# Attention and a squared-ReLU feed-forward layer on one core: q loaded in 1 KB rows, and two more products done with seven half-size products for eight

## The chip, the cores and the metric

The kernel runs on one core of a Trainium2 chip. The metric is the time of one execution on the device in microseconds (us), as the median of several runs. A profile of one execution gives the rest: a core has TensorE (PE; its weight loads are listed as PEld), VectorE (DVE), ScalarE (ACT), GpSimd (POOL), SyncE (SP), which here only issues transfers, and sixteen DMA engines. PE writes to PSUM, which here is cut into two double banks, `strip0` and `strip1`, and four single banks, `ps0` to `ps3`.

## What is computed

The reference, cut to what matters (B = H = 8, S = 576, 16 beacon tokens, D = 64, 4608 tokens, d_model = 512, d_ff = 2048):

```python
k_all = np.concatenate([beacon_k, k], axis=2)          # 592 keys
v_all = np.concatenate([beacon_v, v], axis=2)
scores = scale * np.matmul(q, k_all.transpose(0, 1, 3, 2))
scores = np.where(causal, -1000000000.0, scores)       # beacons are always seen
a = softmax(scores)
x = np.matmul(a, v_all).transpose(0, 2, 1, 3).reshape(4608, 512)
h = np.maximum(x @ w_in, 0.0)
out = (h * h) @ w_out
```

## The kernel before

**Attention.** It goes batch by batch (eight batches), and within a batch by four pairs of heads. Scores are computed with keys on the partitions and queries along the columns (`score_mm`, line 676): the two heads of a pair lie on partitions 0 to 63 and 64 to 127, so a pair's two matmuls use the two halves of the array side by side. `SEGS` lists the causal pieces of a pair (key tile, first and last query), 1664 columns in all. They are put one after the other into strips of 512 columns (`add_stream`), ACT takes the exponential from PSUM into `pt` (line 786), DVE masks the diagonal tiles (line 808), PE multiplies by V with a column of ones (A.V, line 830), DVE divides (lines 848 and 850) and writes `xn`.

**Loads.** For batches 2 to 7 (`b >= NPE`) q, k and v are loaded from SP in tiles of 128 tokens by 8 heads (`add_load`, line 440), in rows of 64 floats, which are 256 bytes. There are six buffers `stg`. POOL casts them to bf16 (line 396), and DMA transposes, issued from SP (`add_trans`, line 472), bring 20 tiles of 128 x 128 of q and as many of k into `qT` and `kT`. Batches 0 and 1 load from POOL's queue or, for the very first tokens, from SP and ACT (`add_first_loads`, line 583), and are transposed by PE. `xn` becomes `xT` by PE for batches 0 to 2, and by DMA transposes from SP (line 882) for the others. `xT` is a ring of 1728 tokens.

**Feed-forward.** The 4608 tokens are nine chunks of 512. A chunk's first product is x by w_in (64 matmuls of 512 columns, line 1143; a chunk that crosses the ring's end has each matmul split in two), then ReLU (lines 1159 and 1161) and square (lines 1169 and 1171). Its second product is by w_out. There are two forms of each:

- Plain. The second product in this form is on line 1194, for chunks below `FAST` = 2.
- Seven for eight. The matrices are cut in quarters and seven products of half size take the place of eight, after sums of quarters made by DVE. For the second product (line 1257) this holds for chunks 2 to 8; the sums of the activations are on line 1228, the evacuations on lines 394 and 1281, the differences of weights on line 944. For the first product it holds for chunks from `BOTH` = 7 on, that is 7 and 8 (`add_first_both`, matmuls on line 1017). POOL copies the chunk out of `xT` (`pull`), DVE makes four sums of it (line 995) and once four of w_in (line 959). One chain of four products (`x`: 1, 6, 7, 4) runs in a strip, read out between the products by ACT or DVE (line 394), the others (`z`: 2; `y`: 5, 3) in a `ps` bank, read out by DVE additions (line 1065). ReLU and square follow on lines 1090 to 1098. These products use memory of the attention: the sums of w_in and the pulled chunk lie in `qk_area`, which holds q and k of the last batches, others in `pt` and `stg`.

**What sets the order.** Each step is an `Op` with a priority, dependencies, and the buffers it takes and gives back. `Order.run` plays a plan of the engines in which every op has a length, and puts the instructions of each engine down in the order that comes out; at run time each engine works its list in that order. Tables refine the plan: `NUDGE` shifts priorities by name, `HOME` fixes an engine. A chunk's ops are added after the batch that completes its tokens (`late`, at the end). The streams of scores are held back by how far the feed-forward work has come (`gate_at`), so that the two kinds of work are interleaved on PE: attention keeps ACT, DVE and the DMA engines busy while PE works on chunks.

Of the kernel before, what the change touches and what calls it, by code (L numbers as in the profile page):

```python
# [17 lines left out]
    "fldk0": 658.071, "fldk1": 538.534, "fcq3": -23.8, "bkl0": 22.188, "ek0.0.0": -25.42, "tp0.0.1k": -476.9,  # L18
    "eq0.0.3": -51.138, "tp0.1.0k": -975.238, "eq0.1.0": -201.003, "tp0.1.1k": 92.697, "ek0.1.1": -17.465,
    "tp0.1.2k": -1278.23, "ek0.1.3": -50.758, "eq0.1.3": 210.345, "qk2.1.0": -1322.85, "qk3.1.0": -1576.95,  # L20
    "qk3.1.2": 98696.4, "xte0.0.1": 72.837, "xte0.0.2": 202.007, "xtp0.1.1": 1543.7, "xtp0.1.3": 299.523,
    "tp1.0.0k": -36.734, "tp1.0.2q": 99521.3, "tp1.0.3k": 99518.5, "mask4.0.2": -52.183, "exp5.7.-1.1.0": -4.503,
    "exp5.7.0.0.0": 466.023, "qk6.10": 99505.4, "exp6.10.-1.0.0": 90.776, "exp6.10.-1.1.0": 79.415,
    "exp6.10.1.0.1": 147.224, "exp7.13.-1.1.0": -161.243, "xte1.0.2": 65.923, "s1.0.0.0": -97989.7,
    "relu0.0.0": 0.295, "s1.0.1.0": -98820.7, "relu0.0.1": 179.265, "sq0.0.1": 54.421, "s1.0.2.0": -300.425,
    "s1.0.3.0": -98822.7, "s1.0.2.1": -118.835, "s1.0.3.1": 8.01, "relu0.3.1": -97.929, "sq0.1.1": -91.845,
    "s1.0.8.1": -99593.7, "sq0.4.1": -12.447, "s1.0.11.0": -100291.234, "relu0.10.1": -97.474,
    "s1.0.11.1": -100375.057, "sq0.5.1": -107.919, "sq0.2.0": -108.607, "s1.0.4.1": 45.995, "s1.0.5.1": -257.73,
    "s1.0.6.0": -12.465, "s1.0.7.0": 328.542, "s1.0.6.1": 126.896, "relu0.6.1": 736.189, "s1.0.12.0": -261.69,
    "s1.0.12.1": -260.74, "s1.0.13.1": -30.691, "s1.0.15.0": 310.934, "sq0.7.0": 214.775, "s1.0.14.1": -78.077,  # L30
    "s1.0.15.1": -476.91, "relu0.15.1": 417.533, "s2.0.1.0": 341.138, "s2.0.2.1": 207.549, "s2.0.3.2": 112.672,
    "s1.1.0.0": 108.494, "s1.1.8.0": 54.353, "s1.1.10.0": 53.3, "s1.1.11.0": 94.01, "s1.1.7.0": 463.778,
    "relu1.7.0": 14.618, "s1.1.12.0": 963.577, "ev1.0": -9.252, "st2": 304.472, "s2.1.2.0": 154.455,
    "s2.1.3.2": 256.085, "ev1.3": -16.524, "av8.0.0": 100447.244, "exp9.7.0.0.0": 31.254, "qk10.10": -1291.46,
    "exp10.10.-1.1.0": -214.735, "relu2.0.0": -393.283, "s1.2.1.0": 160.98, "s1.2.8.0": 1108.37, "s1.2.9.0": 1253.63,
    "s1.2.10.0": -101520.500, "relu2.10.0": -9.869, "s1.2.11.0": -99.215, "s1.2.5.0": -101090.066,
    "s1.2.6.0": -100738.217, "s1.2.7.0": -100723.318, "sq2.3.0": -5.02, "s1.2.12.0": -100712.441,
    "s1.2.13.0": -102656.973, "s1.2.14.0": -102349.519, "s1.2.15.0": 239.8, "sum2.4.0": 1465.92, "sum2.3.0": 1466.01,
    "sum2.3.1": 1606.78, "s2.2.1.1": 823.901, "s2.2.5.0": 76.569, "st5": 565.41, "qk12.5": -1133.88,
    "exp12.5.0.0.0": 293.348, "qk13.8": -830.36, "exp14.11.-1.0.0": -65.743, "exp14.11.-1.1.0": 564.369,  # L40
    "mask14.0.1": -1428.96, "norm15.0.0": 218.979, "xt3.1": 8.184, "xt3.3": 202.161, "s1.3.2.0": 16.151,
    "relu3.2.0": 24.317, "s1.3.10.0": -27.427, "s1.3.11.0": 295.381, "s1.3.5.0": 22.355, "sq3.2.0": -7.233,
    "s1.3.7.0": 5.062, "sq3.3.0": 38.235, "s1.3.15.0": 105.093, "sum3.4.0": 2134.7, "s2.3.2.1": -101383.148,
    "s2.3.6.0": -101211.097, "ev3.u2.None": 150.941, "s2.3.4.1": -101244.799, "st7": 333.885, "qk16.2": 101478.821,
    "exp16.5.0.0.0": 448.591, "av18.0.0": 101516.209, "av18.0.1": 101561.876, "av19.0.0": 101281.365, "xt4.0": 2.246,
    "xt4.3": 248.657, "s1.4.0.0": 1038.21, "s1.4.1.0": -912.296, "s1.4.2.0": 57.023, "sq4.1.0": 11.294,
    "s1.4.8.0": 22.523, "s1.4.9.0": -907.487, "s1.4.11.0": 97.493, "sq4.5.0": -5.964, "s1.4.4.0": -101628.248,
    "s1.4.5.0": 124.134, "s1.4.6.0": 259.779, "relu4.7.0": -11.452, "s1.4.12.0": -102373.044, "relu4.12.0": -342.413,
    "sq4.6.0": 2063.88, "s1.4.14.0": -102369.452, "s2.4.2.0": -102160.747, "s2.4.6.0": 1139.26, "s2.4.5.0": 1742.19,
    "ld5k0": -144.81, "ld5k1": 108.018, "ld5v3": -131.083, "exp20.2.1.0.0": 2412.05, "qk20.5": -126.513,  # L50
    "av20.0.1": 601.406, "exp21.8.0.0.0": -36.383, "exp22.11.0.0.0": -3.784, "xt5.2": 229.366, "xt5.3": 136.903,
    "xt5.4": 110.02, "s1.5.0.0": 35.934, "s1.5.1.0": 178.108, "s1.5.2.0": -1138.86, "relu5.2.0": 7.05,
    "s1.5.3.0": 135.127, "sq5.1.0": -15.732, "s1.5.9.0": -1205.53, "s1.5.11.0": -647.533, "s1.5.4.0": 4.138,
    "s1.5.6.0": 127.935, "s1.5.7.0": -102665.329, "relu5.7.0": -5.3, "s1.5.13.0": 1028.46, "sq5.6.0": 95.713,
    "s1.5.15.0": 365.66, "s2.5.6.1": -102540.099, "s2.5.4.1": -102308.653, "ld6q2": 240.402, "tr6k": -117.387,
    "ld6v0": -220.207, "ld6v1": -231.765, "ld6v2": 23.728, "exp24.2.1.0.0": 20.556, "qk24.5": -215.651,
    "exp24.5.-1.0.0": -166.742, "av24.0.0": 102704.684, "av25.0.0": 102763.978, "exp26.11.-1.0.0": 299.914,
    "xt6.1": 154.988, "xt6.3": 265.679, "s1.6.0.0": 1862.08, "s1.6.1.0": 1656.3, "s1.6.2.0": 868.136,
    "relu6.2.0": -22.081, "s1.6.8.0": 10.058, "relu6.8.0": 18.852, "s1.6.9.0": -103734.110, "sq6.4.0": -332.773,
    "s1.6.10.0": -103829.821, "relu6.10.0": 326.623, "s1.6.11.0": -97.927, "relu6.11.0": 31.773, "relu6.4.0": 42.741,  # L60
    "s1.6.6.0": -103698.974, "s1.6.7.0": -581.885, "s1.6.12.0": 60.655, "s1.6.13.0": -41.185, "relu6.13.0": -218.8,
    "relu6.15.0": -324.763, "sum6.4.1": 177.924, "s2.6.7.0": 1165.61, "ev6.u3.None": -28.927, "s2.6.4.1": 2162.64,
    "ld7q4": 33.222, "ld7v2": 112.962, "ld7v4": 152.964, "qk28.5": -420.296, "exp28.5.-1.1.0": 231.981,
    "mask28.0.0": 2691.56, "exp29.8.-1.1.0": 68.674, "exp30.11.-1.0.0": -314.871, "exp30.11.0.0.0": -315.423,
    "exp30.11.0.0.1": -313.054, "qk31.13": 102124.597, "xt7.0": -229.759, "s1.7.0.6": -899.49, "s1.7.0.7": 1016.51,
    "s1.7.0.20": -104119.166, "s1.7.0.50": -66.869, "s1.7.0.30": -832.088, "s1.7.0.21": -958.553,
    "s1.7.0.51": 974.194, "sq7.0.00": 59.755, "relu7.0.10": -5.01, "relu7.0.11": -1.47, "s1.7.1.1": -873.538,
    "s1.7.1.6": -983.885, "s1.7.1.20": -40.299, "s1.7.1.21": 196.468, "relu7.1.01": 109.61, "sq7.1.01": -28.166,
    "sq7.1.11": 55.47, "sum7.1.1": -202.257, "s2.7.2.0": 912.685, "s2.7.5.1": 1296.88, "s2.7.4.0": 1339.65,
    "xsum8.1": 215.859, "s1.8.0.1": -1300.71, "h8.0.c1": -36.926, "h8.0.u2": -108.725, "s1.8.0.4": 900.706,  # L70
    "s1.8.0.20": 10.275, "h8.0.c110": -203.93, "s1.8.0.50": -1927.81, "s1.8.0.21": 365.361, "s1.8.0.51": 135.258,
    "sq8.0.10": 111.703, "s1.8.1.20": -25.178, "h8.1.c110": -94.403, "s1.8.1.50": 20.17, "s1.8.1.21": -0.349,
    "h8.1.c111": -45.509, "s1.8.1.51": -1.323, "sq8.1.00": 27.394, "relu8.1.01": 103.791, "sq8.1.10": -86.019,
    "sq8.1.11": -42.561, "s2.8.1.1": -901.272, "s2.8.7.0": -193.547,
}

HOME = {
    "fcq3": "ACT", "ek0.0.0": "ACT", "eq0.0.3": "ACT", "eq0.1.0": "ACT", "ek0.1.1": "ACT", "ek0.1.3": "DVE",
    "xte0.0.1": "ACT", "xte0.0.2": "ACT", "xte1.0.2": "DVE", "relu0.0.0": "DVE", "relu0.0.1": "ACT", "sq0.0.1": "ACT",
    "relu0.3.1": "ACT", "sq0.1.1": "ACT", "sq0.4.1": "ACT", "relu0.10.1": "ACT", "sq0.5.1": "ACT", "sq0.2.0": "ACT",  # L80
    "sq0.7.0": "DVE", "relu0.15.1": "ACT", "relu1.11.0": "ACT", "relu1.7.0": "ACT", "ev1.0": "ACT", "ev1.1": "ACT",
    "ev1.3": "ACT", "relu2.0.0": "ACT", "relu2.10.0": "ACT", "sq2.3.0": "DVE", "relu3.2.0": "ACT", "sq3.2.0": "ACT",
# [38 lines left out]
class Order:  # L121
# [22 lines left out]
    def run(self):  # L144
        engines = ["PE", "ACT", "DVE", "POOL", "SP", "-"]
# [115 lines left out]
def kernel(  # L261
# [11 lines left out]
    nc = tc.nc  # L273
# [6 lines left out]
    NT = 5  # L280
# [10 lines left out]
    def sb(name, shape, dt):  # L291
        return pool.tile(shape, dt, name=name)

    FAST, FAST_PE = 2, 0.9
    BOTH = 7
    NSTG, NPT, RB = 6, 3, 3
    PW = 1664
# [1117 lines left out]
```

## Time and profile before

| | us |
|---|---|
| median of 3 runs | 328.89 (328.74 to 329.46) |
| the profiled execution, as timed | 329.39 |
| its span in the profile | 327.5 |
| granted TensorE clock, mean over the span | 0.999 |
| first matmul starts | 5.42 |
| last A.V ends | 255.5 |
| last matmul ends | 323.8 |
| last load of v issued by SP | 233.67 |

| transfers, from the profile's issues | number, KB each | median us to landing |
|---|---|---|
| `stg<-in_q_dram`, 128 tokens | 24, 256 | 4.4 |
| `stg<-in_k_dram`, 128 tokens | 18, 256 | 4.9 |
| `stg<-in_v_dram`, 128 tokens, from SP | 18, 256 | 4.5 |
| `qT<-qk_area` (transpose) | 6 | 6.7 |
| `kT<-qk_area` (transpose) | 6 | 5.6 |
| `xT<-xn` (transpose) | 25 | 3.5 |

How to read the profile: each group has a line of the kernel, an engine, the operation, the target and the sources (buffer numbers left out), the shapes, the number of instructions; then busy time and the mean of one in ns; then the idle time of that engine just ahead of them, and what ended it. The rows in 40 slices show each engine's busy share in tenths. Waits name who waited for whom: us in total, times, longest. A matmul's length in the groups holds its way through the array, which overlaps the next one; what a matmul costs in a row of them is the distance between their starts.

### The profile page before, as it was taken

The numbers are of one execution on the slowest core, as the hardware profiler recorded it, in microseconds if no ns is written. First come the engines' busy times: TensorE is split into PE (matmuls) and PEld (weight loads), VectorE is DVE, ScalarE is ACT, GpSimd is POOL, SyncE is SP. The second block draws the span as 40 slices with busy tenths as digits, with TensorE's granted clock in tenths as the row PEclk, the third lists the DMA queues.
The fourth block names the chain that finished last, engine by engine and source line by source line (L and its number), as shares of the span: only waits on it lengthen the run. The fifth ranks groups of instructions, "written<-read, shape, count | busy, mean of one in ns | idle before, by whom it ended". The sixth has DMA issues, their size and how long they took to land.

```text
span 327.5 us, 8706 instructions
## 1 busy us (share of the span) xinstructions
PE 313.8 (96%) x3558; PEld 226.9 (69%) x3582; DVE 231.9 (71%) x487; ACT 225.9 (69%) x332; POOL 98.0 (30%) x149
## 2 busy tenths in 40 slices
PE   1999999999999999999989999999999999999995
PEld 0468675644565558888966565766788788888884
DVE  3677885525565899576963788678865797897871
ACT  3877796458774984777676888767837664695931
POOL 9854721404533440424033412531200350000000
PEclk9999999999999999999999999999999999999999
DMA  9999997999999999999999999997903210110043
GB/s 157 219 203 212 206 177 140 207 222 205 207 186 192 241 208 182 163 225 237 197 138 217 230 180 200 215 198 156 215 19 130 46 28 2 70 61 0 2 149 111
DMA packets 145602, 51.98 MB, mean 159 GB/s; under 512 B 132506, under 2 KB 140570, under 8 KB 145562
## 3 DMA queue, kind: packets, MB, share of 16 engines
q1 hardware_dynamic: 135901, 42.32, 67.1%
q0 software_dynamic: 8512, 8.49, 15.5%
q10 hardware_dynamic: 1149, 0.62, 0.9%
q8 instruction: 28, 0.46, 0.6%
q14 instruction: 12, 0.10, 0.1%
HBM read 37.22 MB, written 9.44 MB: 142 GB/s over the span
## 4 chain that ended last, share of the span: by engine, by line
PE 81%; DMA 10%; SPq 3%; DVE 2%; ACT 1%; issue 1%; POOL 0%; ACTq 0%; DVEq 0%; POOLq 0%
PE ps L1143 25%; PE ps L1257 19%; PE ps L830 8%; PE ps L1194 8%; PE strip L679 6%; PE strip L1017 4%; PE ps L1017 3%; DMA stg<-in_k_dram 3%; PE strip L1257 2%; DMA kT<-qk_area 2%; DMA osb<-in_q_dram 2%; PE ps L550 2%; PE ps L679 2%; DMA out_dram<-osb 2%; SPq L882 1%; PE ps L899 1%
## 5 line engine op out<-in xcount | busy, mean ns | idle before, releaser
L1143 PE MATMUL ps<-xT,w_in 128*128 128x512 bf16 (+6 forms) x624 | 105.2, 314 | 1.7 <-DMA xT<-xn 0.9
L1143 PEld LDWEIGHTS <-w_in 128*128 128x128 bf16 x640 | 56.2, 98 | 34.9 <-issue 1.4
L786 ACT ACTIVATE pt<-strip 128x1024 bf16<-128x1024 f32 (+3 forms) x77 | 69.6, 956 | 7.8 <-PE strip L679 7.7
L1159 ACT ACTIVATE g<-ps 128x512 bf16<-128x512 f32 (+2 forms) x82 | 44.5, 552 | 20.2 <-PE ps L1143 17.4
L396 POOL CAST qk_area<-stg 128x512 bf16<-128x512 f32 (+2 forms) x60 | 38.2, 642 | 54.7 <-DMA stg<-in_k_dram 28.5
L396 POOL CAST vb<-stg 128x512 bf16<-128x512 f32 (+1 forms) x38 | 27.5, 730 | 83.4 <-DMA stg<-in_v_dram 69.7
L808 DVE TENSOR_TENSOR pt<-pt,tri 128x512 bf16<-128x512 bf16 (+1 forms) x93 | 38.4, 429 | 16.2 <-ACT pt L786 14.9
L1257 PEld LDWEIGHTS <-g 128*128 128x128 bf16 x448 | 42.9, 98 | 7.0 <-issue 0.8
L830 PEld LDWEIGHTS <-pt 128*128 128x128 bf16 x930 | 35.2, 99 | 6.9 <-issue 1.2
L1257 PE MATMUL ps<-w_out,g 128*128 128x256 bf16 x304 | 38.0, 273 | 0.0
L830 PE MATMUL ps<-vb,pt 128*128 128x65 bf16 x930 | 37.6, 196 | 0.0
L1161 DVE TENSOR_SCALAR g<-ps 128x512 bf16<-128x512 f32 (+2 forms) x46 | 27.9, 607 | 12.9 <-PE ps L1143 12.5
L1257 PEld LDWEIGHTS <-sum_area 128*128 128x128 bf16 x336 | 32.0, 98 | 5.8 <-issue 1.8
L850 DVE TENSOR_TENSOR xn<-ps,rcp 128x320 bf16<-128x320 f32 (+2 forms) x64 | 31.5, 492 | 2.6 <-DVE rcp L848 0.4
L394 ACT COPY osb<-ps 128x512 f32<-128x512 f32 x26 | 15.2, 586 | 25.6 <-PE ps L1257 19.2
L1171 DVE TENSOR_TENSOR g<-g 128x1024 bf16<-128x1024 bf16 (+2 forms) x35 | 23.1, 666 | 10.6 <-ACT g L1159 9.9
L1194 PE MATMUL ps<-w_out,g 128*128 128x512 bf16 x120 | 30.0, 379 | 0.4
L679 PEld LDWEIGHTS <-kT 64*128 64x128 bf16 x618 | 20.0, 95 | 14.1 <-issue 10.2
L679 PE MATMUL strip<-qT,kT 64*128 64x128 bf16 (+14 forms) x500 | 29.3, 246 | 0.4 <-ACT qT L394 0.2
L1169 ACT ACTIVATE g<-g 128x1024 bf16<-128x1024 bf16 (+2 forms) x29 | 26.8, 943 | 2.6 <-DVE g L1161 1.8
L786 ACT ACTIVATE pt<-ps 128x512 bf16<-128x512 f32 x42 | 23.4, 599 | 5.6 <-PE ps L679 3.9
L1257 PE MATMUL ps<-w_sum,sum_area 128*128 128x256 bf16 x208 | 26.2, 273 | 0.2 <-ACT osb L394 0.2
(91 smaller groups left out, 356.3 us busy)
## 6 DMA issues: line engine op xcount, KB each, us to landing
out_dram<-osb SPq DMA_DIRECT2D x16, 512.0 KB, 3.7
stg<-in_q_dram SPq DMA_DIRECT2D x24, 256.0 KB, 4.4
stg<-in_k_dram SPq DMA_DIRECT2D x18, 256.0 KB, 4.9
stg<-in_v_dram SPq DMA_DIRECT2D x18, 256.0 KB, 4.5
w_in<-in_moe_w_in_dram POOLq DMA_DIRECT2D x4, 512.0 KB, 12.2
w_out<-in_moe_w_out_dram POOLq DMA_DIRECT2D x4, 512.0 KB, 11.3
stg<-in_v_dram POOLq DMA_DIRECT2D x6, 256.0 KB, 8.6
stg<-in_k_dram SPq DMA_DIRECT2D x6, 224.0 KB, 3.9
```

Of the source, the lines that this page charges most:

```text
L396: eng[e].tensor_copy(dst, src)
L679: nc.tensor.matmul(st[hj][:, at:at + t1 - t0], kT[b % 2][hp, pr, 128 * c:128 * c + 128], qT[b % 2][hp, pr, t0:t1], start=True, stop=True,)
L786: nc.scalar.activation(out, in_, AF.Exp, bias=0.0, scale=scale)
L808: nc.vector.tensor_tensor(out=d, in0=d, in1=tri[0:rows, m0:m0 + m, 0:w][:, None].to_broadcast([rows, 2, m, w]), op=ALU.min)
L830: nc.tensor.matmul(a[:, at + (t - tl[0]) * (D + 1):at + (t - tl[0] + 1) * (D + 1)], P[0:rr, hj, o:o + 128], vb[b % 2][0:rr, c, 2 * pr + hj ...
L850: nc.vector.tensor_tensor(out=xn[b % 2].rearrange("p t (h d) -> p h t d", d=D)[:, h0:h0 + nh, tl[0]:tl[0] + nt], in0=a[:, :, :, 0:D], in1= ...
L1143: nc.tensor.matmul(h[:, lo - spans[0][0]:hi - spans[0][0]], w_in_sb[:, mc, ft * 128:(ft + 1) * 128], xT[:, mc, lo % RING:lo % RING + hi - lo],
L1159: nc.scalar.activation(dst, h, AF.Relu, bias=0.0, scale=1.0)
L1161: nc.vector.tensor_scalar(out=dst, in0=h, scalar1=0.0, scalar2=None, op0=ALU.max)
L1169: nc.scalar.activation(d, d, AF.Square, bias=0.0, scale=1.0)
L1194: nc.tensor.matmul(o, G[:, fc, ts * 128:(ts + 1) * 128], w_out_sb[:, fc, :], start=(fc == 0), stop=(fc == NFT - 1))
L1257: nc.tensor.matmul(o, lhs[:, f, t * 128:(t + 1) * 128], rhs[:, f], start=fresh and f == 0, stop=f == HF - 1, skip_group_check=True)
```

## The change

- `FAST` goes from 2 to 1: the second product of chunk 1 takes the form with seven products.
- `BOTH` goes from 7 to 6: so does the first product of chunk 6. Its ops are added with the last batch, and its chains `z` and `y` now wait for all A.V of the last batch (`probs`), as in chunks 7 and 8.
- For batches 2 to 7, q beyond the first 64 tokens of a head is loaded with four tokens to a row (1 KB), two heads to a transfer. The first 64 tokens of all heads are a fifth transfer in rows of 256 bytes. POOL's cast brings the heads of a pair together; the transposes are one of 16 tiles of 128 x 128 and one of four tiles of 64 rows. `qT` then holds four groups of 128 columns for a pair, one for each place of a token in its row of four, and the first 64 tokens behind them. `score_mm` reads the queries in an order that puts runs of four such columns together, so that PSUM holds each sixteen queries in the order (place in the row, row); a piece that crosses token 64 becomes two matmuls. The exponential reads PSUM in steps, so that `pt` is as before. Where a strip holds the end of one place in `pt` and the start of another, each head has its own exponential.
- Part of the memory that the unused rows of q took is no longer set to zero.
- The first loads of batch 0 are in another order: on SP the beacon rows ahead of k; on ACT the q of pairs 2 and 3 ahead of that of pair 1.
- The lengths in the plan are other numbers, and the tables `NUDGE` and `HOME` are other ones throughout, so each engine's list changes in many places.

The counts of instructions that follow from it, before and after: matmuls 3582 and 3662; ACT's exponentials of `add_stream` 119 and 131; DMA transposes from SP 37 and 43.

```diff
-    FAST, FAST_PE = 2, 0.9
-    BOTH = 7
+    FAST, FAST_PE = 1, 0.9
+    BOTH = 6
...
-    qb = [qk_area[:, (2 * i) * W:(2 * i + 1) * W].rearrange("p (g c d) -> p g c d", g=HP, c=NT)
-          for i in range(2)]
+    PACK, HEAD = 4, S - 512
+    WQ = HP * PACK * 128
+    qb = [qk_area[:, (2 * i) * W:(2 * i) * W + WQ].rearrange("p (g s e) -> p g s e", g=HP, s=PACK) for i in range(2)]
+    qb_head = [qk_area[0:HEAD, (2 * i) * W + WQ:(2 * i + 1) * W].rearrange("p (g e) -> p g e", g=HP) for i in range(2)]
...
+    qT_all = [qT[i].rearrange("p g t -> p (g t)") for i in range(2)]
+    qT_pack = [qT_all[i][:, 0:WQ].rearrange("p (g t) -> p g t", t=128) for i in range(2)]
+    qT_head = [qT_all[i][:, WQ:WQ + HP * HEAD].rearrange("p (g t) -> p g t", g=HP) for i in range(2)]
...
-            nc.gpsimd.memset(qb[b % 2][:, :, NT - 1, :], 0.0)
...
+            if packed:
+                return [queue.dma_start(
+                    out=stg_all[:, ld.held[2]].rearrange("p (u e) -> p u e", u=2),
+                    in_=t[b, 2 * c - 2:2 * c, HEAD:S, :].rearrange("u (p s) d -> p u (s d)", s=PACK))]
...
+            elif packed:
+                copy_on(e, qb[b % 2][:, c - 1].rearrange("p s (u d) -> p s u d", u=2),
+                        stg_all[:, ld.held[2]].rearrange("p (u s d) -> p s u d", u=2, s=PACK))
...
+        def emit_pack(e):
+            nc.sync.dma_start(out=qT_pack[b % 2], in_=qb[b % 2].rearrange("p g s e -> p (g s e)"), transpose=True)
+
+        def emit_head(e):
+            nc.sync.dma_start(out=qT_head[b % 2], in_=qb_head[b % 2].rearrange("p g e -> p (g e)"), transpose=True)
...
-        for lo, hi in ((0, 1), (1, 2), (2, HP)):
-            for n, (x, t) in enumerate((("k", k), ("q", q))):
+        for lo, hi, n in ((0, 1, 1), (2, HP, 0), (2, HP, 1), (1, 2, 0), (1, 2, 1), (0, 1, 0)):
+            for x, t in ((("k", k), ("q", q))[n],):
...
+    def queries(b, hp, pr, t0, t1):
+        if b < NPE:
+            return [(qT[b % 2][hp, pr, t0:t1], 0, t1 - t0)]
+        parts = []
+        if t0 < HEAD:
+            n = min(t1, HEAD) - t0
+            parts.append((qT_head[b % 2][hp, pr, t0:t0 + n].rearrange("p (n i s) -> p n s i", i=4, s=PACK), 0, n))
+        if t1 > HEAD:
+            lo = max(t0, HEAD)
+            parts.append((qT_pack[b % 2][hp, PACK * pr:PACK * pr + PACK, (lo - HEAD) // PACK:(t1 - HEAD) // PACK].rearrange(
+                "p s (n i) -> p n s i", i=4), lo - t0, t1 - t0))
+        return parts
...
-        for hj in range(2):
-            hp = slice(64 * hj, 64 * hj + 64)
-            nc.tensor.matmul(
-                st[hj][:, at:at + t1 - t0],
-                kT[b % 2][hp, pr, 128 * c:128 * c + 128],
-                qT[b % 2][hp, pr, t0:t1],
-                start=True, stop=True,
-            )
+        halves = [queries(b, slice(64 * hj, 64 * hj + 64), pr, t0, t1) for hj in range(2)]
+        for k in range(len(halves[0])):
+            for hj in range(2):
+                rhs, lo, hi = halves[hj][k]
+                nc.tensor.matmul(st[hj][:, at + lo:at + hi], kT[b % 2][64 * hj:64 * hj + 64, pr, 128 * c:128 * c + 128],
+                                 rhs, start=True, stop=True)
...
+                    apart = b >= NPE and len(runs) > 1 and len(hjs) > 1
+                    each = [(*run, h) for run in runs for h in ([(0,), (1,)] if apart else [hjs])]
...
+                            if b >= NPE:
+                                out = out.rearrange("p h (n i s) -> p h n i s" if len(hjs) == 2 else "p (n i s) -> p n i s", i=4, s=4)
+                                in_ = in_.rearrange("p h (n s i) -> p h n i s" if len(hjs) == 2 else "p (n s i) -> p n i s", i=4, s=4)
...
-                        deps=deps + done_g + (exps if chain == "x" else []),
+                        deps=deps + done_g + (exps if chain == "x" else probs),
...
-            if min(((j + 1) * TCH - 1) // S, B - 1) == b:
+            if (min(((j + 1) * TCH - 1) // S, B - 1) if j < BOTH else B - 1) == b:
```

## Prediction

> **What bounds the kernel now.** I read the page first, then PE's waits, the table by stage, the chain that ended last, and the groups with their shapes kept apart. From the page:
>
> ```profile
> span 327.5 us, 8706 instructions
> ...
> PE 313.8 (96%) x3558; PEld 226.9 (69%) x3582; DVE 231.9 (71%) x487; ACT 225.9 (69%) x332; POOL 98.0 (30%) x149
> ...
> PE   1999999999999999999989999999999999999995
> ...
> DMA  9999997999999999999999999997903210110043
> ...
> DMA packets 145602, 51.98 MB, mean 159 GB/s; under 512 B 132506, under 2 KB 140570, under 8 KB 145562
> ```
>
> PE is busy in every slice after the first. The DMA row is as full up to slice 30 (some 246 us), and nearly all its packets are small. Two resources could set the pace there; PE's waits say which one does:
>
> ```profile
> PE ps L547 <- ACT qk_area L394: 5.6, 2, 5.4
> PE ps L1143 <- DMA xT<-xn: 0.9, 1, 0.9
> ...
> PE ps L679 <- DMA kT<-qk_area: 0.4, 1, 0.4
> ```
>
> After the start (5.6) PE waited only 1.3 us for transfers. DMA is full but ahead. Busy time alone does not show a full array, because matmuls overlap, so I took PE's rate from the chain (start, us, what):
>
> ```profile
> 55.67 1.73 PE ps L1194 x8
> ...
> 255.53 6.99 PE ps L1143 x64
> ...
> 288.43 1.75 PE strip L1017 x16
> ```
>
> A matmul of 512 columns takes 1.73/8 = 0.216 us, one of 256 takes 1.75/16 = 0.109 us: the time is the columns. From 28 us on, hardly 2 us are idle. A product saved on PE is therefore time saved, if the other engines keep up. By stage (length; PE, PEld, DVE, ACT, POOL busy; clock, DMA share, GB/s):
>
> ```profile
> 28.00:249.00 221.00, 218.16 (x2565) 149.03 (x2588) 155.77 (x328) 158.56 (x236) 71.25 (x106) 1.00 1.04 188
> 249.00:256.00 7.00, 7.00 (x111) 5.47 (x105) 4.23 (x11) 5.50 (x10) 0.00 (x0) 1.00 0.40 152
> 256.00:263.00 7.00, 7.00 (x68) 5.11 (x66) 4.99 (x9) 5.21 (x8) 3.28 (x4) 1.00 0.37 75
> 263.00:323.00 60.00, 60.00 (x551) 53.65 (x550) 49.13 (x84) 37.91 (x49) 3.95 (x4) 1.00 0.13 46
> ```
>
> The last stage is seven-product work alone, and PE never pauses in it with DVE at 49.1 of 60 us.
>
> **The change part by part.**
>
> *Second product of chunk 1.* 64 matmuls of 512 columns go (64 x 0.216 = 13.8 us) and 7 x 2 x 8 = 112 of 256 come (112 x 0.109 = 12.2): **-1.6 us** of PE. It adds four DVE sums on two halves each (8 x 0.74 = 5.9 us) and more evacuations; the weight differences (four of 1.21 us) come one chunk earlier. DVE has 221 - 156 = 65 us free in that stage.
>
> *First product of chunk 6.* Now it is 64 matmuls of 384 and 64 of 128 columns, because the chunk crosses the ring's end. Half of them are the 6.99 us in the chain, so 13.98 us go and 12.2 come: **-1.7 us**. It also moves. The products of this form wait for all scores of batch 7 (chain x) or all its A.V (the others), so it can no longer fill PE during that attention. Counted in columns by the order of the instructions, PE's work ahead of the last A.V falls from 225.8 to 219.1 us, so attention must finish 6.7 us sooner: near 249 instead of 255.5.
>
> *The q loads.* Of 4608 packets of 256 B per batch, 4096 become 1024 of 1 KB. The packet records give 18 ns for the median of 256 B on this queue and 46 ns for 1 KB (stores; no 1 KB load is there). That is (4096 x 18 - 1024 x 46)/16 = 1.7 us of sixteen engines per batch; the transposes lose 256 of 5120 rows, 0.3 us. Six batches: 12 us of DMA. By the 23 ns mean of the 256 B packets it would be 20; if 1 KB cost four times 18, nothing. On PE it is worth nothing directly: this pays for the 6.7 us above. If the cover is gone, a batch waits for its transposes. SP issues one more transpose per batch, but 16 tiles and four half tiles take the place of 20, at some 0.2 us a tile (3.3 to 5.1 us in the trace). The xT transposes and v loads queued behind it move little. POOL loses two memsets of 0.52.
>
> *Scores.* The packed rows leave the queries in another order. PE now reads them in runs of four at steps of 128 elements (the first 64 tokens of a head: single elements, four apart), and the exponentials put the order right while reading PSUM. Segment 0 is split at token 64: 24 x 2 more matmuls. The start times give 102 ns for two heads' 240 columns, 28 for 64 and 75 for 176: +1 ns a split, **0.0**. For ACT the rows answer:
>
> ```profile
> L786 ACT ACTIVATE pt<-ps 128x512 bf16<-128x512 f32 x42 | 23.4, 599 | 5.6 <-PE ps L679 3.9 <-DVE pt L808 1.7
> ...
> L1159 ACT ACTIVATE g<-ps 128x512 bf16<-128x512 f32 x64 | 37.8, 599 | 17.0 <-PE ps L1143 14.7 <-DVE rcp L848 1.9
> ...
> L394 ACT COPY xT<-ps 128x240 bf16<-128x240 bf16 x3 | 1.0, 363 | 0.8 <-PE ps L899 0.8
> ...
> L394 ACT COPY qT<-ps 128x240 bf16<-128x240 bf16 x2 | 0.7, 356 | 0.2 <-PE ps L547 0.2
> ```
>
> The ReLU reads every second column and costs as much as the straight exponential; the qT copy hops 120 elements at each step and costs as much as the straight xT copy. So the stepped read is free on ACT. Where a strip holds two runs, heads part: 12 more exponentials, 2.3 us in all from 256 columns at 0.40 and 512 at 0.61, beside 62 us in which ACT is free before 249.
>
> For PE no row reads the moving operand in steps. The streams of batches 2 to 7 are 24 pairs x 1664 columns at 2.4 a ns = 16.6 us. [...] I take 0, after the nearest rows, the two ACT pairs above, and keep the other end as a rival. [...]
>
> *Start.* The beacon rows are loaded first, and on ACT's queue the large q load goes ahead of the second small one. PE's first transpose waits for the first q load as before (5.42). PE starts at 5.4 us and has some 13 us of gaps up to 28; I cost the new order at 0, within 1 either way.
>
> *Stalls.* The 1.3 us of DMA waits may go with lighter loads; the denser end may bring others. I take 0, from -1.3 to +3.
>
> **Sum:** -1.6 - 1.7 + 0.0 = -3.3; I round to -3.2 for the splits' extra instructions. The profiled execution took 329.39 us (span 327.5 and 1.9 around it): 326.2. It lies 0.5 above the median of 328.89, so I predict **325.7**.
>
> **The rivals.**
>
> *A, PE's columns decide* (the forecast): 323.8 to 327.3, the sum with its start and ordinary stalls. For it: no idle PE over 295 us. Chance **0.62**.
>
> *B, slower: the stepped queries slow PE's stream.* Place: every score matmul of batches 2 to 7. Price: 16.6 us at half speed, so 342; the break-even is 3.2/16.6, a stream 19% slower. For it: no row shows such a read, and PE has no slack to hide it. Against it: the ACT rows. [...] Chance **0.14**, 329.6 to 342.
>
> *C, chunk 6 has lost its place.* Its first product now stands almost alone: 120 matmuls, 13.1 us, with no other product between. It needs 8 strip reads of 1.02 (8.2 us), 12 adds of 0.686 (8.2) and ReLU and squares of about 12 us, half of what lines 1090 to 1098 took for two chunks: 28.4 us on two engines, so 14.2 each, against 13.1 of PE. The sums of weights and inputs (4 x 1.25 and 4 x 0.52) come on DVE just before. If the tail of this does not fit under the following products, or batch 7 is late, PE loses 1.5 to 5 us: 327.3 to 331. Against it: ReLU and squares can run under chunk 7, and chunk 8 shows a block of 9.6 us of this kind without a pause. Chance **0.16**: 0.04 still faster, 0.05 the same, 0.07 slower.
>
> *D, more is gained:* the DMA waits go and the start gains up to 1 us: 322.5 to 323.8. Chance **0.08**.
>
> That the packets do not get cheaper is inside C: batch 7 would then be late by up to 6.7 us less the present lead.
>
> **How the numbers follow.** Faster by over 0.2% (under 328.2; that is about what the measurement tells from no change): 0.62 + 0.08 + 0.04 = 0.74. Same: 0.05. Slower: 0.14 + 0.07 = 0.21. The range leaves out most of B and the edge of D: 322.8 to 331.0. The forecast alone is 323.8 to 327.3.
>
> **What will show it.** Right: the score pairs of 240 columns, or 64 and 176, still take about 102 ns; exponentials of 512 columns stay at 599 ns; 256-column matmuls follow at 109 ns in chunk 1 and chunk 6; 1 KB loads cost near 46 ns; the last A.V ends near 249; PE idles under 3 us after 28. Wrong: the score stream over 120 ns for 240 columns (B); PE waiting for ACT or DVE around 245 to 265, or for kT and qT (C).

## The result, and the profile after

The changed kernel takes 338.14 us (median of 4 runs, 337.45 to 339.0) against 329.17 for the kernel before beside it (4 runs, 328.74 to 329.51). The ratio is **1.027, 95% interval 1.024 to 1.03: slower**, by about 9 us where 3.2 were to be gained. (In all ratios, runs over 1.5% above the fastest of the same kernel are left out; medians are of all runs.) The page of the profiled execution (338.3 us as timed):

```profile
span 336.6 us, 8928 instructions
...
PE 313.4 (93%) x3640; PEld 234.5 (70%) x3662; DVE 249.2 (74%) x511; ACT 234.8 (70%) x347; POOL 104.6 (31%) x155
...
PE   2999999999978999999889999899989979999995
...
DMA  9999979999999999499969999880613400030033
...
DMA packets 125827, 51.60 MB, mean 153 GB/s; under 512 B 106586, under 2 KB 120794, under 8 KB 125786
```

The PE row has holes from slice 12 (93 to 101 us) on, where before one slice between the first and the last was under 9; the DMA row has got somewhat thinner, as it should (from 28 to 249 us its share fell from 1.04 to 0.93). By stage, in the windows that the prediction used (length; PE, PEld, DVE, ACT, POOL busy):

```profile
28.00:249.00 221.00, 209.23 (x2535) 146.22 (x2556) 162.76 (x329) 159.84 (x245) 78.72 (x112) 1.00 0.93 186
249.00:256.00 7.00, 7.00 (x88) 6.37 (x86) 4.46 (x14) 1.20 (x3) 0.00 (x0) 1.00 0.01 2
...
263.00:323.00 60.00, 58.12 (x528) 51.47 (x527) 53.01 (x89) 48.37 (x58) 5.80 (x8) 1.00 0.11 35
```

From 28 to 249 us PE stands still for 221 - 209.2 = 11.8 us; before it was 2.8. The stage that rival C pointed at, from 249 on, adds 2 us. DVE is busy 162.8 of 221 us, with 58 to spare. PE's waits after the start name it first all the same:

```profile
PE ps L872 <- DVE pt L850: 3.2, 6, 1.4
PE ps L720 <- DVE xn L892: 1.6, 2, 1.2
PE ps L1059 <- POOL pt L402: 1.4, 2, 0.9
PE ps L1299 <- ACT osb L400: 1.0, 2, 0.7
```

(L872 is A.V, L850 the masks, L720 the scores.) In the chain that ended last PE falls from 81% of the span to 53%, and DVE rises from 2% to 19%.

Counted from the starts of the matmuls, PE's columns fell by 3.2 us (293.9 to 290.7), as the sum had it. All of the loss is standing still, some 15 us more of it than before: the 9 us, the 3.2 us of columns, and 2.6 us that PE had gained by 30 us and lost again. After 28 us there are 13 stands of over 0.5 us, 10.8 us together; before there were 2, 1.6 us together. The rest are shorter ones. (A start counts as late by what it exceeds the columns of the matmul ahead; this is the measure "stands" in the table below.)

**One hole read closely.** ACT's timeline and PE's around the longest stand (start, us, what; in brackets the idle time ahead and what ended it):

```profile
89.42 0.59 ACT L400 COPY osb<-ps 128x512 f32<-128x512 f32 x1 [1.78 <-PE ps L1299]
93.56 0.59 ACT L400 COPY osb<-ps 128x512 f32<-128x512 f32 x1 [3.55 <-PE ps L1299]
95.59 1.08 ACT L828 ACTIVATE pt<-ps 128x512 bf16<-128x512 f32 x2 [1.45 <-PE ps L720]
```

```profile
95.39 0.63 PE L720 MATMUL strip<-qT,kT 64*128 64x144 bf16 x16
95.96 1.05 PE L1299 MATMUL ps<-w_sum,g 128*128 128x256 bf16 x8
96.84 1.91 PE L1299 MATMUL ps<-w_out,sum_area 128*128 128x256 bf16 x16
100.13 0.63 PE L872 MATMUL ps<-vb,pt 128*128 128x65 bf16 x15 [1.39 <-DVE pt L850]
```

The wait is put down to DVE, but DVE's own timeline shows it idle for 2.1 us just before 97.0, with nothing to do, and for 0.9 before 99.4, waiting for ACT; and ACT had been idle for 3.6 and 1.5 us, waiting for PE. PE's list holds chunk 1's second product (L1299) almost in one piece, nine half products between two groups of scores; ACT has nothing to exponentiate, and when the product is through, PE waits while exponentials, masks and A.V follow one after the other. So the profile itself suggests the **order** of the lists (theory O below). The rival is the **load** that the two products add to DVE and ACT (theory L). A third theory, that the packed q costs by itself (theory Q), is tested along with them.

### The profile page after: what moved, and what is told of

Same layout as the page of the kernel before. It is cut to its first block, busy times and chain, and to the rows that moved or that the text cites. A ratio compares the mean times of both kernels' runs of the same rounds, so it can differ in the third digit from the quotient of the medians.

```text
span 336.6 us, 8928 instructions
## 1 busy us (share of the span) xinstructions
PE 313.4 (93%) x3640; PEld 234.5 (70%) x3662; DVE 249.2 (74%) x511; ACT 234.8 (70%) x347; POOL 104.6 (31%) x155
## 3 DMA queue, kind: packets, MB, share of 16 engines
q1 hardware_dynamic: 116125, 41.92, 58.7%
## 4 chain that ended last, share of the span: by engine, by line
PE 53%; DVE 19%; DMA 12%; ACT 8%; POOL 3%; issue 3%; DVEq 0%; ACTq 0%; POOLq 0%
PE ps L1299 19%; PE ps L1185 13%; ACT pt L828 6%; PE strip L1059 5%; DMA qk_area<-in_q_dram 5%; DVE sum_area L1270 5%; PE ps L872 4%; DMA w_out<-in_moe_w_out_dram 4%; PE ps L1059 4%; PE ps L1236 3%; DVE pt L850 3%; PE strip L720 2%; PE strip L1299 2%; DMA w_in<-in_moe_w_in_dram 2%; DMA out_dram<-osb 2%
## 5 line engine op out<-in xcount | busy, mean ns | idle before, releaser
L1185 PE MATMUL ps<-xT,w_in 128*128 128x512 bf16 (+3 forms) x494 | 90.4, 324 | 2.3 <-DVE rcp L890 0.6
L1185 PEld LDWEIGHTS <-w_in 128*128 128x128 bf16 x512 | 46.6, 98 | 30.3 <-issue 3.7
L402 POOL CAST qk_area<-stg 128x512 bf16<-128x512 f32 (+2 forms) x60 | 42.2, 719 | 52.4 <-DMA stg<-in_k_dram 30.1
L1299 PEld LDWEIGHTS <-g 128*128 128x128 bf16 x512 | 48.4, 98 | 9.5 <-issue 2.5
L1201 ACT ACTIVATE g<-ps 128x512 bf16<-128x512 f32 (+2 forms) x68 | 36.3, 540 | 22.0 <-PE ps L1185 20.6
L850 DVE TENSOR_TENSOR pt<-pt,tri 128x512 bf16<-128x512 bf16 (+1 forms) x93 | 37.1, 418 | 14.8 <-ACT pt L828 14.4
L1299 PE MATMUL ps<-w_out,g 128*128 128x256 bf16 x352 | 45.1, 273 | 0.4 <-DVE g L1107 0.2
L872 PEld LDWEIGHTS <-pt 128*128 128x128 bf16 x930 | 35.5, 98 | 11.2 <-DVE pt L850 4.1
L1299 PEld LDWEIGHTS <-sum_area 128*128 128x128 bf16 x384 | 37.1, 98 | 7.8 <-issue 2.6
L872 PE MATMUL ps<-vb,pt 128*128 128x65 bf16 x930 | 38.9, 194 | 3.3 <-DVE pt L850 3.2
L720 PEld LDWEIGHTS <-kT 64*128 64x128 bf16 x666 | 21.2, 95 | 15.8 <-issue 12.1
L1299 PE MATMUL ps<-w_sum,sum_area 128*128 128x256 bf16 x240 | 30.0, 273 | 1.2 <-ACT osb L400 0.7
L720 PE MATMUL strip<-qT,kT 64*128 64x80 bf16 (+15 forms) x548 | 29.4, 237 | 1.2 <-ACT kT L400 0.5
L1213 DVE TENSOR_TENSOR g<-g 128x1024 bf16<-128x1024 bf16 (+2 forms) x26 | 17.4, 668 | 13.8 <-ACT g L1201 13.4
L1323 DVE TENSOR_TENSOR osb<-ps,osb 128x512 f32<-128x512 f32 (+1 forms) x26 | 16.7, 644 | 9.9 <-PE ps L1299 6.4
```

The costliest lines, as they stand in the source:

```text
L402: eng[e].tensor_copy(dst, src)
L720: nc.tensor.matmul(st[hj][:, at + lo:at + hi], kT[b % 2][64 * hj:64 * hj + 64, pr, 128 * c:128 * c + 128], rhs, start=True, stop=True)
L850: nc.vector.tensor_tensor(out=d, in0=d, in1=tri[0:rows, m0:m0 + m, 0:w][:, None].to_broadcast([rows, 2, m, w]), op=ALU.min)
L872: nc.tensor.matmul(a[:, at + (t - tl[0]) * (D + 1):at + (t - tl[0] + 1) * (D + 1)], P[0:rr, hj, o:o + 128], vb[b % 2][0:rr, c, 2 * pr + hj ...
L1185: nc.tensor.matmul(h[:, lo - spans[0][0]:hi - spans[0][0]], w_in_sb[:, mc, ft * 128:(ft + 1) * 128], xT[:, mc, lo % RING:lo % RING + hi - lo],
L1201: nc.scalar.activation(dst, h, AF.Relu, bias=0.0, scale=1.0)
```

## The experiments

All comparisons are ratios to the kernel before, run on the same chip. The chips differ: on some the kernel before spread over 327 to 333 us, so intervals are 0.2 to 0.6% either way. The granted clock was 0.997 or more in most runs. In 6 of the 12 of `after_slack_order`, 4 of the 10 of `packed_q_alone` and 15 of the 24 of the last two kernels of the table it was 0.987 to 0.995, and these runs took longer, by the medians 2.4 to 3.8 us for each kernel; why is not known. Where it matters, the others are given by themselves.

| kernel | median us | ratio, 95% interval | profiled span | stands after 28 us: number, us |
|---|---|---|---|---|
| changed kernel | 338.14 | 1.027, 1.024 to 1.03 | 336.6 | 13, 10.8 |
| `after_new_order` | 334.52 | 1.008, 1.0046 to 1.0114 | 333.5 | 7, 6.4 |
| `packed_q_alone` | 334.2 | 1.0073, 1.0036 to 1.0111 | 329.8 | 4, 3.9 |
| `before_new_order` | 333.61 | 1.008, 1.0041 to 1.0119 | 331.7 | 5, 5.7 |
| `chunk6_plain` | 340.09 | 1.0266, 1.021 to 1.0322 | 339.3 | 10, 10.0 |
| `short_sums_chunk1` | 336.83 | 1.0231, 1.0186 to 1.0276 | 334.0 | 11, 9.9 |
| `short_sums_chunks1to5` | 333.46 | 1.0149, 1.0096 to 1.0202 | 330.8 | 8, 7.4 |
| `packed_and_chunk6` | 331.96 | 1.0086, 1.0056 to 1.0115 | 330.4 | 3, 2.6 |
| `packed_and_chunk1` | 331.5 | 1.0076, 1.0047 to 1.0105 | 328.3 | 5, 3.4 |
| `after_slack_order` | 327.97 | 0.9953, 0.9922 to 0.9983 | 325.5 | 2, 4.6 |
| `packed_chunk1_slack_order` | 327.24 | 0.9929, 0.9897 to 0.9961 | 324.5 | 2, 1.8 |
| `packed_q_slack_order` | 327.56 | 0.9939, 0.991 to 0.9967 | 327.7 | 2, 2.0 |
| `before_slack_order` | 328.09 | 0.9954, 0.9929 to 0.9978 | 326.1 | 0 |
| `after_slack_order_2` | 327.27 | 0.9928, 0.9893 to 0.9963 | 325.2 | 1, 0.6 |
| `packed_chunk6_slack_order` | 327.9 | 0.9957, 0.993 to 0.9985 | 325.4 | 2, 1.3 |
| `packed_q_slack_order_2` | 328.47 | 0.9979, 0.9953 to 1.0006 | 326.4 | 3, 2.3 |
| `slack_order_short_sums` | 325.4 | 0.9877, 0.9841 to 0.9914 | 323.1 | 1, 1.3 |
| `both_products_plain_q_slack` | 330.51 | 1.0008, 0.9967 to 1.0049 | 326.6 | 2, 2.4 |
| `packed_chunk1_slack_order_2` | 329.37 | 0.9963, 0.9924 to 1.0001 | 324.7 | 1, 1.1 |

### Another order for the same instructions

`after_new_order` changes only the tables (with them some evacuations, ReLUs and squares go from ACT to DVE or back):

```diff
 NUDGE = {
-    "ek0.0.2": -27.363, "eq0.0.3": 0.207, "tp0.1.1k": -919.621, "tp0.1.1q": -995.46, "cast0v4": 299.177,
+    "ident": 414.90948700779524,
+    "tri": 364.9070237858176,
...
```

> The changed kernel, every instruction as it is, with other tables NUDGE and HOME: a random search shifted priorities and swapped ACT and DVE, and kept what lets the written plan end sooner. So only the order of each engine's list, and the engine of some evacuations, differ. Theory O (the order written down is the cause: the same work fits, but PE stands behind DVE at places where the list puts DVE's work late): 326 to 331 us, and PE's idle time between 90 and 290 us falls from about 15 us to under 8. Theory L (load: the sums, additions and readouts of the two products overfill DVE and ACT, whatever the order): 335 to 339, with the same 15 us. Theory Q (the packed q costs by itself): 335 to 339 as well.

Two kernels with tables of the same search, on other instructions (`FAST = 2`, `BOTH = 7` in the changed kernel; the kernel before as it is):

> The changed kernel with FAST = 2 and BOTH = 7 again, so with packed q alone, and tables searched in the same way. Theory L: as fast as before or faster, 326 to 329.5, since DVE has its old load. Theory Q: 333 to 338. Theory O: 3 us above after_new_order by PE's columns, so 329 to 334.

> The kernel before, with tables searched in the same way: the control for the search. If such tables are as good as those the kernel had, 327 to 331. Theory O says more: the order alone, with every instruction kept, can move the time by several us, so 331 or more is possible. Theories L and Q say nothing of it but that it stays within 1 us of 329.

And part of the change undone without touching the tables:

```diff
-    BOTH = 6
+    BOTH = 7
```

> The changed kernel with BOTH = 7 again, the tables as they stand: chunk 6's first product is plain and comes before the end of attention. PE has 1.7 us more columns. Theory L: 332 to 336, since the block of readouts at 256 to 275 us is gone. Theory O: no better, 337 to 343, since the tables were made for the other list. Theory Q: about 339 to 340, the columns alone.

`after_new_order` is 1.9% faster than the changed kernel (1.008 against 1.027) with every product in place: theory O's direction, though at 334.5 us it falls short of its 326 to 331. Theories L and Q, which expected no gain from another order, both fail on it. `packed_q_alone` is level with it (theory O had expected 3 us more), and so is the control: from this search all three come out at 1.008, whatever products they have. So the kernel before has a better order than this search finds, the changed kernel a worse one. `chunk6_plain` gains nothing from having chunk 6 out of the way (1.0266), as theory O said.

### Less work for DVE in the same order

The sums of chunk 1's activations are made on one block of 256 columns instead of four; the rest of the sum is left out:

```diff
-                    nc.vector.tensor_tensor(out=o[:, fs], in0=a[:, fs], in1=c[:, fs], op=op)
+                    r = slice(fs.start, fs.start + 1) if j == 1 else fs; nc.vector.tensor_tensor(out=o[:, r], in0=a[:, r], in1=c[:, r], op=op)
```

> The changed kernel, every engine's list in the same order, but chunk 1's eight sums of activations work on 256 of their 1024 columns (so chunk 1's second product is computed from incomplete sums); six small memsets on POOL in an idle gap at 43 us give the rest of the area a value. DVE does about 4 us less between 83 and 95 us. Theory D (DVE's sums stand ahead of the masks of batch 2, and PE waits for these): PE's idle time between 90 and 110 us, 6 us in the changed kernel, falls by 2 to 4, and the time to 334 to 336.5. Theory E (PE waits there for ACT's exponentials or for x of batch 2, and DVE is not what is late): within 1 us of the changed kernel, 337 to 339.

With `j < 6` for `j == 1`:

> The same for chunks 1 to 5, all that is done during attention: about 22 us less of DVE, all lists in the same order (the second products of these chunks are computed from incomplete sums). Theory D: the waits for DVE up to 235 us go, and the idle time of 35 us up to 170 us and 44 at 250 falls by 5 to 8 us: 330 to 333. Theory E: 336 to 339. If the gain is that of short_sums_chunk1 and no more, only the new sums hurt, not those that the kernel before had as well.

The first gives 0.4%, some 1.3 us, which the intervals do not tell from nothing; the two stands at 98 and 102 us shrink only from 1.6 and 0.8 to 1.1 and 0.8. That fits the reading above: there the exponentials were late, not DVE. With the sums of five chunks short, 1.2% or 4 us come back, and the stands fall from 10.8 to 7.4. So DVE's sums do hold PE up, and mostly those that the kernel before had too. But DVE then does less in all than in the kernel before (229.2 us busy against 231.9):

```profile
PE 312.5 (94%) x3662; PEld 234.0 (71%) x3662; DVE 229.2 (69%) x511; ACT 234.4 (71%) x347; POOL 100.7 (30%) x161
```

and this order still stays 1.5% above it. The load of DVE does not explain the loss.

The two products one at a time, each with tables from the search:

> The changed kernel with FAST = 2 again (chunk 1's second product plain), tables searched as for after_new_order. Theory P (in orders of the same quality the product in chunk 1 costs more than its 1.6 us, for DVE's sums stand in PE's way; chunk 6's product gains its 1.7): ratio to before 1.000 to 1.005, that is below packed_q_alone and after_new_order. Theory C (chunk 6 alone at the end is what costs): 1.008 to 1.014.

> The changed kernel with BOTH = 7 again (chunk 6's first product plain and during attention), tables searched in the same way. Theory P: ratio to before 1.008 to 1.013, the worst of the searched ones. Theory C: 1.000 to 1.006.

1.0086 and 1.0076: neither P nor C. No single product carries the loss.

### Orders that leave room

The first search kept what let the written plan end sooner; on the chip its orders came out at 1.008 or so. A second search judged an order by how it stands when every length varies by some 10%, and counted DVE's operations on SBUF half as long again while POOL casts (in the changed kernel masks of 512 columns took 598 ns for 416, sums of 1024 took 1070 for 684). The two additions were not tried apart. Again only the tables differ.

> The changed kernel, every instruction as it is, with tables from a second search: an order now counts by how it stands when every length varies by about 10%, and when DVE's operations on SBUF take half as long again while POOL casts, as the traces show (masks 416 and 598 ns, sums 684 and 1030 to 1092). Theory S (both products do give their 3.3 us of columns, but only where the order leaves DVE room): ratio to before 0.988 to 1.000, 2 to 4 us below packed_q_slack_order, PE's idle time within 1 us of that kernel's. Theory L (what the products save in columns is lost again in waits for DVE and ACT, in any order): within 1 us of packed_q_slack_order or above it.

> The changed kernel with BOTH = 7 (chunk 6's first product plain), tables from the second search. Theory S: half way between after_slack_order and packed_q_slack_order, 1.5 us from each. Theory L: within 1 us of both; or, if chunk 1's sums alone are what costs, above packed_q_slack_order.

> The changed kernel with FAST = 2 and BOTH = 7, packed q alone, tables from the second search. If packed q itself costs nothing: ratio to before 0.995 to 1.005. If it costs by itself: 1.008 or more, as in packed_q_alone.

> The kernel before, tables from the second search, the control. If the second search is better than the first, ratio 0.992 to 1.003 where before_new_order had 1.008. Theory S: after_slack_order lies 1 to 3 us below this one; theory L: level with it or above.

The changed kernel's own work now takes 327.97 us, 0.9953 of the kernel before: **10 us came from the tables alone**, that is from the order and from which of ACT and DVE does some of the steps (ACT 226.5 us busy instead of 234.8 over the whole kernel, DVE 249.2 in both). The two were not varied apart. The control, the kernel before in such an order, is as fast (0.9954). By stage, `after_slack_order`:

```profile
28.00:249.00 221.00, 216.42 (x2686) 153.63 (x2684) 168.59 (x352) 157.84 (x244) 78.41 (x112) 1.00 0.91 189
```

PE is busy for 216.4 us in place of 209.2, while DVE does more in this window than in the changed kernel (168.6 against 162.8) and ACT about as much. So DVE was not too full; its work was placed badly. Attention ends at 249.1 us here, where the prediction had it. PE's list around chunk 1's second product shows what moved (each entry is half a product, numbered as in the kernel, or a group of scores; A.V and transposes between them are left out):

```
changed kernel               1 1  scores  2 5 6 2 6 5 7 7 4  scores  4 3 3  A.V, scores, A.V
after_slack_order    scores  1 2 1 2  scores  6 5 6 5 7 7 4 4 3  scores  3  chunk 2's first product
after_slack_order_2  scores  1 1 2  scores  2 6 5 6 5 7 7 4 4  scores  3 3  scores, chunk 2's first product
```

The second group of scores, which stood behind eleven half products with its A.V right after the last, stands behind four or three, and after the product PE has chunk 2 to go on with. `packed_q_slack_order` (0.9939) settles theory Q: the packed q costs nothing by itself. But theory S (both products give their 3.3 us where the order leaves DVE room) is only half right. The kernels with and without the two products are equal within their intervals, as theory L had it, and PE still stands once for long:

```profile
PE ps L1299 <- ACT osb L400: 4.3, 2, 2.8
```

The timelines of DVE, POOL and ACT there:

```profile
84.09 2.11 DVE L1270 TENSOR_TENSOR sum_area<-g 128x1024 bf16<-128x1024 bf16 x2
86.12 1.70 DVE L1270 TENSOR_TENSOR sum_area<-sum_area,g 128x1024 bf16<-128x1024 bf16 x2
...
88.34 2.11 DVE L1270 TENSOR_TENSOR sum_area<-g,sum_area 128x1024 bf16<-128x1024 bf16 x2
...
90.97 0.56 DVE L850 TENSOR_TENSOR pt<-pt,tri 80x160 bf16<-80x160 bf16 x2
```

```profile
83.72 2.96 POOL L402 CAST qk_area<-stg 128x512 bf16<-128x512 f32 x3 [0.39 <-DMA stg<-in_k_dram]
```

```profile
91.63 1.02 ACT L828 ACTIVATE pt<-strip 128x1024 bf16<-128x1024 f32 x1 [3.08 <-DVE pt L850]
```

Here it is DVE: seven of chunk 1's eight sums in a row, 1.09 us each in five beside POOL's casts and 0.68 in the other two, hold back the masks to 90.97; ACT's exponential waits 3.1 us for them, the read-out of the product stands behind that exponential, and PE waits 2.75 us for the read-out.

### What eats the two products' gain

> The changed kernel once more, every instruction as it is, with tables from a second pass of the search with slack, from another start of the random numbers. If the result of after_slack_order (ratio 0.995) is a property of such orders and no stroke of luck: 0.990 to 1.000. Theory S: below packed_q_slack_order_2 by 2 to 4 us. Theory L: within 1 us of it or above.

> The changed kernel with FAST = 2 (chunk 1's second product plain, chunk 6's first product with seven products), tables from the search with slack. It fills the fourth place beside packed q alone (0.9939), with chunk 1 (0.9929) and with both (0.9953). Theory S: 0.988 to 0.993. Theory L: 0.993 to 0.999. If chunk 6, and not chunk 1, is what eats the gain: above 0.996.

> Packed q alone, tables from the second pass of the search with slack. It shows how far two orders of equal standing lie apart: within 1.5 us of packed_q_slack_order (0.994) if the search decides little, further if the order is a lottery of several us.

> The kernel of after_slack_order with all lists in the same order, but chunk 1's eight sums on 256 of 1024 columns (its second product is computed from incomplete sums; six small memsets on POOL in an idle gap). In after_slack_order these sums fill DVE from 84 to 90 us, the masks behind them start at 91.0, and PE stands for 2.9 us at 91.8. If they are the price that eats the gain of the two products: PE's stand there goes, and the ratio falls from 0.995 to 0.985 to 0.990. If not: 0.993 to 0.997.

The second order of the changed kernel is as good (0.9928, with one stand of 0.6 us), so 0.995 was no luck. With chunk 1's sums short, the masks start at 88.6 instead of 91.0, the stand at 91.8 us is gone (the longest wait for a read-out, 1.1 us, is another one, at 165 us), and the ratio falls from 0.9953 to 0.9877, with intervals that don't meet. That would be 2.5 us, but part of it goes with the granted clock: the six runs of `after_slack_order` at 0.994 and 0.995 took 328.4 to 330.0 us, the six at 0.998 and above have a median of 327.10, against 325.4 with short sums. So in that order chunk 1's sums cost some 1.7 us, about the 1.6 us of columns that its product saves. `after_slack_order_2` has the same sums without that stand, and at 327.27 is no faster for it: by 30 us its PE had done 1.3 us of columns less than in `after_slack_order`, a loss that the table's stands do not count.

Two more kernels, the first to see what the packed q is worth:

> The kernel before with both products (FAST = 1, BOTH = 6, and chunk 6's ops added and held back as in the change), but q loaded in 256-byte rows as before; tables from the search with slack. The prediction said that the lighter loads of q pay for attention's ending 6.7 us sooner. If so: PE waits for kT, qT or xT in batches 5 to 7, and the ratio is 1.000 to 1.010. If DMA has room enough without them: 0.990 to 0.997, as after_slack_order and after_slack_order_2.

> Packed q and chunk 1's product, tables from the second pass of the search with slack. A second order for the kernel that was the fastest of its group (0.9929): within 0.003 of it if it is better than packed q alone (0.9939 and 0.9979), at 0.996 to 0.999 if that was luck.

With q in 256-byte rows and both products the ratio is 1.0008, 0.7% above the mean of the two kernels with packed q (0.9941). Most of that goes with the granted clock: in eight of the twelve runs it was 0.987 to 0.995, with a median of 331.8 us; in the four at 1.0 the median is 328.89, or 0.9965 of the kernel before at 0.998 and above. `after_slack_order`, counted in that way, has 0.9933. So a gain of some 1 us from packed q would fit, and none is shown. In the profile one wait for a transfer stands out, a wait for `xT` at 176 us and not at the end of attention:

```profile
PE ps L1143 <- DMA xT<-xn: 1.7, 1, 1.7
```

The second order for chunk 1's product gives 0.9963 (0.9943 by its five runs at 0.998 and above) after 0.9929: the gain of that product is not told from none. Over all slack orders with packed q, none of the products has 0.9939 and 0.9979, chunk 1's 0.9929 and 0.9963, chunk 6's 0.9957, both 0.9953 and 0.9928. Both against none, by the means (0.9941 and 0.9959): -0.2%, some 0.6 us, with about 0.3% of uncertainty; the 3.3 us of the sum would be 1.0%. And packed q alone against the kernel before (0.9954), in such orders: no difference.

## Why the prediction was wrong

**The step that failed** is the last of the sum: "Stalls. ... I take 0, from -1.3 to +3." By PE's busy time it was some 9 us between 28 and 249 us alone (2.8 to 11.8) and 2 more behind; by the starts of the matmuls, some 15. The change was said to give "other tables throughout, so each engine's list changes in many places", and no term of the sum, and no rival, stood for that. The runs price it: the changed kernel's work takes 1.027 of the time before with the tables it came with, 1.008, 0.9953 and 0.9928 with three others.

**"A product saved on PE is therefore time saved, if the other engines keep up"** failed at its condition. "DVE has 221 - 156 = 65 us free in that stage" was right as a sum (58 were free) and no answer. What counts is what stands ahead of the masks and read-outs that PE needs next, and whether scores come early enough to keep ACT fed.

Point by point:

- *PE's columns*: -3.2 us, right. In orders of one search about 0.6 of it reaches the time, which is not told from none; chunk 1's sums took some 1.7 us in one of them.
- *Stepped queries (rival B)*: right, nearly free. Two heads' 240 columns went from 102 to 105 ns, 208 from 89 to 92; the split pair of 64 and 176 takes 32 and 82 instead of 28 and 75. Over some 260 pairs that makes about 1 us instead of 0.0. The half speed in rival B's price was the author's assumption, and no run shows it: 240 columns took 3% longer.
- *Exponentials from stepped PSUM*: right, 599 ns for 512 columns before and after, 1029 for 1024 (1032 before).
- *q loads*: the median 1 KB packet takes 47 ns (46 taken; the mean is 58). The queue's share went from 67.1% of 327.5 us to 58.7% of 336.6, 22 us less of sixteen engines (12 taken, 20 by the mean of the packets). What that is worth in time is not shown.
- *Attention's end*: 249 was forecast, 259.1 measured, since PE stood still on the way; 249.1 with the tables of `after_slack_order`.
- *Start*: 0 within 1 was taken; by 30 us PE had done 2.6 us more columns (15.1 against 12.5), and lost them again.
- *Rival C* had the right sign and the wrong place: DVE and ACT at the end of attention. From 249 us on only about 2 us were lost, and `chunk6_plain` was no faster.

**What stays open**: why both products together gain some 0.6 us over packed q alone, and not 3.3. One order shows chunk 1's sums as the price; another has no such stand, loses at the start instead, and is barely faster than one without the products. And whether an order exists that gets all of it wasn't tried further. The fastest complete kernels, `after_slack_order_2` and `packed_chunk1_slack_order`, beat the kernel before by 0.7% (intervals above), and they owe most of it to the order: the kernel before gains 0.5% from the same search.

## What to carry to other kernels

Where a written-out order is replaced along with the work, price the order first: the same work differed by 3.4% here, three times what the saved products could bring, and a fair test of a product needs an order made for each side. A free share of an engine over a long stage says little; look at what its list puts ahead of the short steps that the next engine waits for. And where a wait is put down to one engine, follow it back until an engine is found that wasn't itself waiting: at the changed kernel's longest stand that led from DVE to ACT to PE's own list.

## What the hardware showed besides

DVE's masks and sums, which have two operands in SBUF, stretch while POOL casts. In the changed kernel's records masks of 512 columns take 416 ns (median) with POOL idle and 598 where POOL casts for at least four fifths of their time; sums of 1024 take 684 and 1070. Not every one is hit: those masks lie between 414 and 826 ns, those sums between 678 and 1130. Of the operations that read PSUM, `xn` of 320 columns takes 491 ns in both cases and DVE's ReLU of 512 takes 686 and 685. Even a sum cut to 256 columns, 0.28 us alone, took 0.65 us beside casts (`slack_order_short_sums`). The casts of q and k get longer too: 645 ns on average before, 702 in the changed kernel, which has 64 sums of activations for 56. In the changed kernel they take 606 to 615 ns where no DVE operation with both operands in SBUF is beside them, and 605 to 1101, with a median of 784, where such operations run for at least four fifths of their time. What decides which of them are hit was not followed here.
